# An mLSTM layer and an ELU network on one core: queries and keys as 112 rows, two small copies removed, the order made anew

## The chip, the cores and the metric

One core of a Trainium2 chip runs the whole program. The metric is device time in microseconds (us). The core has five engines with a queue each: TensorE (PE in the profile, and PEld for its weight loads), VectorE (DVE), ScalarE (ACT), GpSimd (POOL) and SyncE (SP), which here issues every transfer. Engines run side by side and wait for each other through semaphores; each works through its own list in order.

## The reference, cut to what matters

For each of 4 x 8 heads a matrix memory is updated step by step over 768 positions; its outputs, 3072 rows of 320 numbers, go through a two-layer network with an ELU between.

```python
# q, k, v, o_gate: (4, 8, 768, 40); i_gate, f_gate: (4, 8, 768)
for t in range(S):
    m_new  = np.maximum(f_gate[:, :, t] + m, i_gate[:, :, t])
    f_stab = np.exp(f_gate[:, :, t] + m - m_new)
    i_stab = np.exp(i_gate[:, :, t] - m_new)
    C = f_stab * C + i_stab * outer(v_t, k_t)          # 40 x 40 per head
    n = f_stab * n + i_stab * k_t
    y[:, :, t] = sigmoid(o_t) * (C @ q_t) / max(abs(n . q_t), 1)
x = y.transpose(0, 2, 1, 3).reshape(3072, 320)
h = x @ w_in                                          # 320 x 2048
g = np.where(h > 0, h, np.exp(np.minimum(h, 0)) - 1)
out = g @ w_out                                       # 2048 x 320
```

## The kernel before, in words

The sequence is cut into 6 chunks of 128 positions; a **tile** is one chunk of one of the 4 batches with its 8 heads, so there are 24 tiles, numbered t0 to t23. For a tile PE forms keys times queries per head (L752, two heads side by side on partitions 0 to 39 and 64 to 103, 16 matmuls). A weight matrix w holds the decays: for the first two chunks PE spreads the sums of logarithms lcs over a tile (L779 to L789, six matmuls for half the heads, "a spread") and ACT takes the exponential (L804); for later chunks DVE makes it with a scan (L796). DVE multiplies w by the products (L813). The outputs come from PE: from the second chunk on the state C times the decayed queries (L833), then w times values (L841), then the addition to the state (L851). The decay comes through DRAM: it is written as b_d and read back spread over 40 partitions into bb (L705), its last column is copied to dec (L769), and bb is multiplied by the queries in place (L770). The state shrinks by dec (L868, two instructions) and takes the addition (L879). The outputs are gated and divided into xf (L899, L903), xf's last 64 columns are copied behind it (L907), PE turns xf (L917), and it is stored as a high and a low part, xh and xl.

Two or three tiles make a **block** (9 blocks). For each block and each of 16 slices of 128 hidden columns, a **step**, PE makes h with eight matmuls (L970), ACT and DVE make the ELU and its two parts gh and gl (L978 to L988), and PE adds to acc (L997). The weights come as 64-bit words and are converted on ACT, DVE and POOL (L429 to L477); wide and narrow are their buffers. The last 64 rows of w_in of two groups share one conversion, "the tail".

Nothing runs in the order of the code. Each piece is given to a planner as an `op` with costs by engine; the planner plays the program through by these costs and a table of ranks (PLACES) and of fixed engines (USES), and writes the instructions of each engine in the order of its own start times. Where PE would stand idle in the plan before 70 us, it puts in matmuls on a tile of ones that nobody reads (L526, "fills"), one for each 0.22 us:

```python
done = self.FIRST_WORK
for t, _, e, o in order:
    if e == "PE":
        if done < t < self.WARM:
            self.fill(max(0, round((t - done - self.SLACK) / 0.22)))
        done = o.end
    o.fn(e)
```

At the very start PE gets EARLY_WORK of them ahead of anything else. The buffers of queries and keys (qk, three), of decays (bb, three) and of h (two, which spreads use as well) are taken in turn.

Of the kernel before, what the change touches and what calls it, by code (L numbers as in the profile page):

```python
# [15 lines left out]
ALU = mybir.AluOpType  # L16
# [4 lines left out]
P = 128  # L21
# [17 lines left out]
class Plan:  # L39
# [52 lines left out]
    def run(self):  # L92
# [17 lines left out]
        engines = {e: 0.0 for o in self.ops for e in o.engines}  # L110
        queue, port, t, order, events, small = 0.0, 0.0, 0.0, [], {0.0}, False
# [95 lines left out]
def tile_mlstm_then_elu_ffn(  # L207
# [9 lines left out]
    nc = tc.nc  # L217
    PSUM = bass.MemoryType.PSUM
    B, NC, _, _, _, HH, L = qk.shape
    D = 40  # L220
    DM, DFF = w_in.shape[1], w_in.shape[0] * w_in.shape[2]
# [21 lines left out]
    EARLY_WORK = 10  # L243
# [8 lines left out]
    room = dict(  # L252
        wide=3, narrow=2, gates=2, qk=3, bb=3, vko=3, w=3, wl=2, dec=2, den=2, xf=2,
        x=3, ps_a=3, h=2, acc=3, e=2, gh=4, gl=4, os=3,
    )
    PLACES = {"clear": 7.1154181, "g0": -0.805181392, "qk0": -0.351178529, "v0":
# [22 lines left out]
    USES = {"clear.2": "POOL", "rows.0": "DVE", "rows.1": "DVE", "rows.2": "DVE",  # L279
        "states.0": "ACT", "states.2": "ACT", "g0.0": "ACT", "g0.7": "DVE", "p0.4": "ACT",  # L280
        "p0.8": "DVE", "y0.6": "DVE", "y0.8": "DVE", "p1.4": "ACT", "p1.10": "POOL", "v1.1":
        "ACT", "y1.6": "ACT", "p2.10": "POOL", "v2.1": "ACT", "p3.4": "ACT", "v3.1": "ACT",
# [4 lines left out]
        "ACT", "g2.2": "DVE", "g2.4": "POOL", "g2.10": "DVE", "p8.3": "ACT", "p8.9": "ACT",  # L287
# [19 lines left out]
        "ACT", "d3.0": "ACT", "d3.1": "DVE", "c4.0": "ACT", "c5.2": "POOL", "c6.1": "ACT",  # L307
# [827 lines left out]
```

## Time and profile before

| | before |
|---|---|
| time, median of 3 runs | 470.45 us (469.73 to 471.0) |
| the profiled execution's own time | 468.6 us |
| its span, first to last instruction | 466.8 us |
| PE busy | 458.5 us, 98% |
| DVE busy | 336.5 us, 72% |
| ACT busy | 277.9 us, 60% |
| POOL busy | 100.6 us, 22% |
| transfers of SP's queue, share of 16 engines | 33.6% |

The time is that of an execution; the span is what the profile covers, 1.8 us less. Busy time counts what an engine runs, fills included, so a high share for PE does not by itself say that all of it is wanted work.

### The profile page before, as it was taken

The numbers are of one execution on the slowest core, as the hardware profiler recorded it, in microseconds if no ns is written. First come the engines' busy times: TensorE is split into PE (matmuls) and PEld (weight loads), VectorE is DVE, ScalarE is ACT, GpSimd is POOL, SyncE is SP. The second block draws the span as 40 slices with busy tenths as digits, with TensorE's granted clock in tenths as the row PEclk, the third lists the DMA queues.
The fourth block names the chain that finished last, engine by engine and source line by source line (L and its number), as shares of the span: only waits on it lengthen the run. The fifth ranks groups of instructions, "written<-read, shape, count | busy, mean of one in ns | idle before, by whom it ended". The sixth has DMA issues, their size and how long they took to land.

```text
span 466.8 us, 13897 instructions
## 1 busy us (share of the span) xinstructions
PE 458.5 (98%) x5737; PEld 429.1 (92%) x5737; DVE 336.5 (72%) x698; ACT 277.9 (60%) x672; POOL 100.6 (22%) x137
## 2 busy tenths in 40 slices
PE   9899999999999999999999999999999999999996
PEld 4557799999999999989999999999999999999996
DVE  7899899899888878778887853587894754354432
ACT  5778678788866456454654565354545455545664
POOL 1226302320212031234111340131041201010011
PEclk9999999999999999999999999999999999999999
DMA  7956374334208361246405501353411301000100
GB/s 210 317 183 198 102 276 146 114 98 148 86 8 236 103 226 41 79 131 199 144 17 150 173 1 43 114 165 119 133 45 38 95 0 44 1 3 0 44 1 28
DMA packets 42175, 49.71 MB, mean 106 GB/s; under 512 B 3360, under 2 KB 34816, under 8 KB 42112
## 3 DMA queue, kind: packets, MB, share of 16 engines
q1 hardware_dynamic: 42112, 48.82, 33.6%
q8 instruction: 45, 0.74, 0.6%
q14 instruction: 18, 0.15, 0.1%
HBM read 43.42 MB, written 5.39 MB: 105 GB/s over the span
## 4 chain that ended last, share of the span: by engine, by line
PE 96%; DVE 2%; ACT 1%; issue 1%; DVEq 0%; ACTq 0%
PE h L970 39%; PE acc L997 36%; PE ps_a L752 6%; PE ps_a L841 3%; PE ps_a L833 3%; PE acc L526 3%; PE ps_a L917 2%; PE ps_a L851 1%; PE h L779 1%; PE h L485 1%; PE h L789 1%; PE h L783 1%; DVE gl L988 0%; DVE w L477 0%; DVE w L813 0%
## 5 line engine op out<-in xcount | busy, mean ns | idle before, releaser
L970 PE MATMUL h<-xh,w 128*128 128x384 f32 (+1 forms) x720 | 176.6, 321 | 0.0
L997 PE MATMUL acc<-w,gh 128*128 128x320 f32 x768 | 172.2, 311 | 0.9 <-ACT den L886 0.7
L997 PEld LDWEIGHTS acc<-w,gh 128*128 128x128 f32 x768 | 128.9, 188 | 2.6 <-issue 0.6
L983 DVE SCALAR_TENSOR_TENSOR e<-e,h 128x384 f32<-128x384 f32 (+1 forms) x144 | 72.7, 505 | 80.6 <-ACT e L981 79.9
L970 PEld LDWEIGHTS h<-xh,w 128*128 128x128 f32 x720 | 124.6, 188 | 1.7
L978 ACT ACTIVATE e<-h 128x384 f32<-128x384 f32 (+1 forms) x144 | 65.4, 454 | 93.3 <-PE h L970 85.4
L997 PE MATMUL acc<-w,gl 128*128 128x320 f32 x384 | 118.7, 309 | 0.5 <-DVE gl L988 0.5
L970 PE MATMUL h<-xl,w 128*128 128x384 f32 (+1 forms) x432 | 111.4, 317 | 0.0
L986 ACT CAST gh<-e 128x384 fp32r<-128x384 f32 (+1 forms) x144 | 68.1, 474 | 39.6 <-DVE e L983 38.5
L970 PEld LDWEIGHTS h<-xl,w 128*128 128x128 f32 x432 | 76.3, 188 | 0.0
L988 DVE TENSOR_TENSOR gl<-e,gh 128x384 fp32r<-128x384 f32 (+1 forms) x109 | 60.6, 558 | 20.0 <-ACT gh L986 19.7
L997 PEld LDWEIGHTS acc<-w,gl 128*128 128x128 f32 x384 | 72.0, 188 | 0.9 <-DVE gl L988 0.9
L981 ACT ACTIVATE e<-e 128x384 f32<-128x384 f32 (+1 forms) x144 | 70.5, 490 | 3.6
L988 POOL TENSOR_TENSOR gl<-e,gh 128x384 fp32r<-128x384 f32 (+1 forms) x35 | 33.5, 956 | 171.2 <-ACT gh L986 125.7
L796 DVE TENSOR_TENSOR_SCAN w<-w,ident 128x512 f32<-128x512 f32 x32 | 39.4, 1241 | 1.5 <-DMA w<-f_d 1.5
L813 DVE TENSOR_TENSOR w<-ps_a,w 128x512 f32<-128x512 f32 x48 | 31.4, 683 | 2.0 <-ACT wl L342 1.0
L752 PE MATMUL ps_a<-qk 40*128 40x128 f32 x384 | 29.9, 291 | 0.3 <-DVE xl L342 0.2
L752 PEld LDWEIGHTS ps_a<-qk 40*128 40x128 f32 x384 | 25.1, 193 | 5.2 <-issue 1.8
L903 POOL TENSOR_TENSOR xf<-xf,den 128x320 f32<-128x320 f32 x13 | 10.8, 831 | 45.0 <-DVE den L891 44.6
L841 PE MATMUL ps_a<-vko,w 128*32 128x41 f32 x1536 | 19.4, 201 | 1.0 <-DVE w L813 0.9
L841 PEld LDWEIGHTS ps_a<-vko,w 128*32 128x32 f32 x1536 | 17.7, 109 | 2.2 <-DVE w L813 1.5
L868 POOL TENSOR_TENSOR C<-C,dec 40x164 f32<-40x164 f32 x20 | 10.0, 498 | 33.2 <-PE ps_a L833 27.2
(114 smaller groups left out, 432.2 us busy)
## 6 DMA issues: line engine op xcount, KB each, us to landing
w<-f_d SPq DMA_DIRECT2D x32, 256.0 KB
vko<-in_vko SPq DMA_DIRECT2D x24, 324.0 KB
qk<-in_qk SPq DMA_DIRECT2D x48, 160.0 KB
wide<-in_w_out SPq DMA_DIRECT2D x8, 640.0 KB
wide<-in_w_in SPq DMA_DIRECT2D x8, 512.0 KB
vko<-in_vko SPq DMA_DIRECT2D x24, 160.0 KB
out<-os SPq DMA_DIRECT2D x24, 160.0 KB
bb<-b_d SPq DMA_DIRECT2D x40, 80.0 KB
```

Source lines behind the costliest of these rows:

```text
L526: nc.tensor.matmul(spare, ones, ones.unsqueeze(1).to_broadcast([P, 4, P]), start=True, stop=True, skip_group_check=True,)
L752: nc.tensor.matmul(ps(two, P, HH, L)[:, j, :], kt[rows, j, :], qt[rows, j, :], start=True, stop=True,)
L796: nc.vector.tensor_tensor_scan(a, a, ident4.rearrange("p h t -> p (h t)"), 0.0, op0=ALU.mult, op1=ALU.add)
L813: lambda e, half=half: nc.vector.tensor_mul(w(half), ps(half, P, HH, L), w(half)),
L841: nc.tensor.matmul(y[r, h, :], w()[:, i, r], va()[:, h, :], start=not opened, stop=(i == H - 1), skip_group_check=True,)
L970: nc.tensor.matmul(h(), a[g][:, fs], m, start=(i == 0), stop=(i == len(prods) - 1))
L978: op(act(N), lambda e, h=h, ff=ff: nc.scalar.activation(ff("e"), h(), AF.Relu, scale=-1.0), (KHP,), (KE,))
L981: lambda e, ff=ff: nc.scalar.activation(ff("e"), ff("e"), AF.Exp, scale=-1.0), (), (KE,))
L983: lambda e, h=h, ff=ff: nc.vector.scalar_tensor_tensor(out=ff("e"), in0=ff("e"), scalar=-1.0, in1=h(), op0=ALU.add, op1=ALU.max),
L986: op(act(N), lambda e, ff=ff: nc.scalar.copy(ff("gh", F32R), ff("e")), (KE,), (KG,))
L988: lambda e, ff=ff: eng[e].tensor_sub(ff("gl", F32R), ff("e"), ff("gh", F32R).bitcast(F32)),
L997: nc.tensor.matmul(acc(a), x[:, sl], bw[g][:, j, :], start=(f == f0 and i == 0), stop=(f == f1 - 1 and i == 2),)
```

## The change

What it does: queries and keys of a tile come in one transfer of 112 rows in place of two of 40 rows; the rows 40 to 63 between the halves are zeros from DRAM, so the three memsets of qk's middle rows go. The tail of w_in comes as one transfer of 128 rows in place of two of 64. The decay times the queries is written into the queries' buffer, so bb stays whole, dec and its copy go, and the state shrinks with one instruction on 104 partitions that reads bb's last column. The gating product is written back into the gates' buffer (v3), and the division writes all 384 columns of xf at once, in the order (part, row, head); the rows of w_in are put in the same order, the copy of 64 columns goes. In the planner RATE, FIRST_WORK, EARLY_WORK, PE's start and a few costs change, and both tables are new; with them the order on all engines.

```diff
-    RATE = 255e3
+    RATE = 290e3
-    FIRST_WORK, WARM, SLACK = 5.0, 70.0, 0.1
+    FIRST_WORK, WARM, SLACK = 6.6, 70.0, 0.1
...
         engines = {e: 0.0 for o in self.ops for e in o.engines}
+        engines["PE"] = self.FIRST_WORK
...
-    EARLY_WORK = 10
+    EARLY_WORK = 13
+    W = 3 * P // (2 * H)
...
-    PLACES = {"clear": 7.1154181, "g0": -0.805181392, "qk0": -0.351178529, "v0":
-    USES = {"clear.2": "POOL", "rows.0": "DVE", "rows.1": "DVE", "rows.2": "DVE",
+    USES = {"clear.0": "DVE", "clear.1": "ACT", "clear.2": "ACT", "states.0": "DVE",
...
-                src = [w_in[x, 2 * P :] for x in (g, g + 1)]
+                src = [w_in[2 * (NF // G) + g // 2]]
...
-        op({"ACT": 0.2 + 0.00092 * n, "DVE": 0.13 + 0.0011 * n}, size, both[1::2], (KN,))
-        op({"ACT": 0.2 + 0.00092 * n, "DVE": 0.13 + 0.0011 * n}, rounding, (), both[0::2])
+        op({"ACT": 0.2 + 0.00092 * n} | one_in, size, both[1::2], (KN,))
+        op({"ACT": 0.2 + 0.00092 * n} | one_in, rounding, (), both[0::2])
...
-        plan.at("rows", rank["t0"])
-        for j, t in enumerate(qks):
-            op({"DVE": 0.52, "POOL": 0.56},
-               lambda e, t=t: eng[e].memset(t[32:64, 0], 0.0), (), (("qkzero", j),))
...
-        for x in range(2):
-            op({"SP": 0.4}, lambda e, x=x: nc.sync.dma_start(t[ROWS[x]], qk[b, c, x]),
-               (("qkzero", n % room["qk"]),), (("qk", n, x),), nbytes=D * 2 * HH * L * 4)
+        op({"SP": 0.4}, lambda e: nc.sync.dma_start(t[0:QR], qk[b, c]),
+           (), (("qk", n, 0), ("qk", n, 1)), nbytes=2 * D * 2 * HH * L * 4)
...
-            op({"POOL": 0.22, "DVE": 0.17, "ACT": 0.2},
-               lambda e: copy(e, dec(), bb[0:R2, :, L - 1 : L]), KB, (("dec", n),))
-            op(two_in(HH * L), lambda e: eng[e].tensor_mul(bb[0:R2], bb[0:R2], qt[0:R2]), KQ, KB)
+            op(two_in(HH * L), lambda e: eng[e].tensor_mul(qt[0:R2], bb[0:R2], qt[0:R2]), KB, KQ)
...
-                            y[r, 2 * j : 2 * j + 2, :], bb[0:R2, j, r], C[b][0:R2, j],
+                            y[r, 2 * j : 2 * j + 2, :], qt[0:R2, j, r], C[b][0:R2, j],
...
-                    for two, rows in enumerate(ROWS):
-                        cv = C[b][rows, :, two, :]
-                        eng[e].tensor_mul(cv, cv, dec()[rows].to_broadcast([D, HH, E]))
+                    cv = C[b][0:R2].rearrange("p j two e -> p j (two e)")
+                    eng[e].tensor_mul(cv, cv, bb[0:R2, :, L - 1 : L].to_broadcast([R2, HH, 2 * E]))
...
-        op(two_in(H * D),
-           lambda e: eng[e].tensor_mul(gated(), gated(), den().to_broadcast([P, H, D])),
-           (("den", n),), (("xf", n),))
-
-        op({"port": 1, "DVE": 0.12, "POOL": 0.25, "ACT": 0.24},
-           lambda e: copy(e, xf()[:, H * D :], xf()[:, 2 * P : H * D]), (), (("xf", n),))
+        def divided(e):
+            y = v3()[2]
+            parts, step = y.ap[0], y.ap[-1][0]
+            twice = bass.AP(
+                tensor=y.tensor, offset=y.offset,
+                ap=[parts, [D * step, H], [(D - W) * step, 2], [step, W]],
+            )
+            eng[e].tensor_mul(
+                xf().rearrange("p (a d h) -> p h a d", a=2, h=H), twice,
+                den().unsqueeze(3).to_broadcast([P, H, 2, W]),
+            )
+
+        op(two_in(3 * P), divided, (("den", n), KS), (("xf", n),))
```

The order of instructions, at three places of the start. **SP's queue**, from its first transfer (gates; vko are values, keys and output gates of a tile, wide a weight's buffer). Before:

```order
L518 DMA gatesfi<-in_gates 32x256
L677 DMA vko<-in_vko 128x648
L671 DMA qk_148<-in_qk 40x1024 x2
L682 DMA vko<-in_vko 128x320
L429 DMA wide<-in_w_in 128x512
L429 DMA wide<-in_w_in 64x512 x2
L671 DMA qk_149<-in_qk 40x1024 x2
```

The same place with the change:

```order
L522 DMA gatesfi<-in_gates 32x256
L672 DMA qk_145<-in_qk 112x1024
L683 DMA vko<-in_vko 128x320
L678 DMA vko<-in_vko 128x648
L433 DMA wide<-in_w_in 128x512 x2
L678 DMA vko<-in_vko 128x648
L672 DMA qk_146<-in_qk 112x1024
```

The first tile's queries and keys now go second, each pair of transfers is one, and the first weight is the fifth transfer in place of the sixth.

**DVE**, where the log sums of the first chunk are split into three parts (lcs) and the first weight's conversion begins (narrow<-wide). Before:

```order
L342 CAST lcs<-gateslc 32x256
L636 TENSOR_TENSOR gateslc<-gateslc,lcs 32x256
L342 CAST lcs<-gateslc 32x256
L636 TENSOR_TENSOR gateslc<-gateslc,lcs 32x256
L342 CAST lcs<-gateslc 32x256
L439 TENSOR_SCALAR narrow<-wide 128x512
```

With the change:

```order
L346 CAST lcs<-gateslc 32x256
L638 TENSOR_TENSOR gateslc<-gateslc,lcs 32x256
L346 CAST lcs<-gateslc 32x256
L443 TENSOR_SCALAR narrow<-wide 128x512
L638 TENSOR_TENSOR gateslc<-gateslc,lcs 32x256
L460 TENSOR_SCALAR narrow<-narrow 128x512
```

The conversion's first instruction, which needs the first weight, now stands ahead of the last step of the log sums, and the third cast has left DVE.

**ACT** at the same time, from the first tanh of the gates (L766) or shortly behind it, through the exponentials of the first tile (w<-h). Before:

```order
L766 ACTIVATE vko<-vko 128x320
L443 ACTIVATE wide<-wide 128x512
L804 ACTIVATE w<-h 128x512
L342 COPY wl<-w 128x4
L804 ACTIVATE w<-h 128x512
```

With the change:

```order
L346 COPY gatesm<-m_120 32x1
L447 ACTIVATE wide<-wide 128x512
L346 CAST lcs<-gateslc 32x256
L441 ACTIVATE narrow<-wide 128x512
L447 ACTIVATE wide<-wide 128x512
L800 ACTIVATE w<-h 128x512 x2
```

The third cast of lcs now stands on ACT behind one conversion instruction of the first weight, and two of the second weight stand ahead of the first tile's exponentials.

## Rows read from the trace of the kernel before

**Rows 1.** The page: span, then busy time and share by engine.
```profile
span 466.8 us, 13897 instructions
...
PE 458.5 (98%) x5737; PEld 429.1 (92%) x5737; DVE 336.5 (72%) x698; ACT 277.9 (60%) x672; POOL 100.6 (22%) x137
```

**Rows 2.** Busy us per engine by stretch (instructions), clock, DMA share, GB/s.
```profile
0.00:10.00 10.00, 8.94 (x31) 4.32 (x32) 7.06 (x24) 5.92 (x14) 1.80 (x10) 1.00 0.76 210
10.00:20.00 10.00, 9.79 (x163) 5.99 (x162) 7.97 (x17) 7.65 (x21) 2.70 (x4) 1.00 0.95 305
20.00:80.00 60.00, 57.47 (x1033) 45.78 (x1031) 54.26 (x118) 45.73 (x113) 19.44 (x27) 1.00 0.60 192
80.00:140.00 60.00, 60.00 (x502) 59.56 (x501) 54.89 (x108) 45.90 (x96) 10.51 (x13) 1.00 0.27 88
140.00:300.00 160.00, 159.20 (x2197) 154.15 (x2196) 117.70 (x244) 86.50 (x230) 39.01 (x54) 1.00 0.38 116
...
460.00:466.80 6.80, 3.12 (x19) 2.44 (x17) 1.34 (x3) 1.63 (x4) 0.74 (x1) 1.00 0.14 48
```

**Rows 3.** The chain in order of time: start us, us, engine, tile, line.
```profile
1.06 4.45 PE acc L526 x10
...
5.51 2.54 PE ps_a L752 x16
...
8.04 2.55 PE acc L526 x6
...
49.45 1.09 PE acc L526 x5
...
165.49 1.59 PE h L970 x8
...
178.65 1.39 PE h L970 x8
```

**Rows 4.** Waits of PE: us in total, times, longest.
```profile
PE ps_a L841 <- DVE w L813: 0.9, 1, 0.9
PE acc L997 <- ACT den L886: 0.7, 1, 0.7
...
PE acc L997 <- DVE gl L988: 0.5, 1, 0.5
```

**Rows 5.** Timeline, first 40 us: start us, us, engine, line, operation.
```profile
7.51 0.28 DVE L342 CAST lcs<-gateslc 32x256 bf16<-32x256 f32 x1
...
9.08 0.68 ACT L443 ACTIVATE wide<-wide 128x512 int32<-128x512 uint32 x1 [2.25 <-DMA wide<-in_w_in]
9.08 0.43 DVE L439 TENSOR_SCALAR narrow<-wide 128x512 int32<-128x512 int32 x1 [1.29 <-DMA wide<-in_w_in]
...
10.43 0.38 PE L779 MATMUL h<-mask,ident_b 128*128 128x512 bf16 x1
...
11.29 0.60 ACT L804 ACTIVATE w<-h 128x512 f32<-128x512 f32 x1 [1.52 <-PE h L789]
...
29.72 0.32 SPq L626 DMA_DIRECT2D b_d<-gatesfi  x1
...
38.40 0.19 POOL L342 COPY dec<-bb 104x4 f32<-104x4 f32 x1 [0.36 <-DMA bb<-b_d]
```

**Rows 6.** Groups by line and form: busy us, mean ns, idle before.
```profile
L903 DVE TENSOR_TENSOR xf<-xf,den 128x320 f32<-128x320 f32 x11 | 5.3, 485 | 0.2
...
L868 DVE TENSOR_TENSOR C<-C,dec 40x164 f32<-40x164 f32 x12 | 4.5, 377 | 0.2
...
L342 ACT COPY xf<-xf 128x64 f32<-128x64 f32 x16 | 3.8, 236 | 3.3 <-DVE xf L903 2.1 <-POOL xf L903 1.2
...
L575 DVE MEMSET qk<- x3: 485/485/485, 1.2 to 2.2; 32x512 f32 x3
```

**Rows 7.** The tile qk: ns min/median/max, first and last start us.
```profile
L752 PE MATMUL ps_a<-qk x384: 266/272/579, 5.4 to 410.7; 40*128 40x128 f32 x192
...
L671 SPq DMA_DIRECT2D qk<-in_qk x48: 281/310/1127, 1.7 to 349.5; - x48
```

More of the change, by code (lines that the diff above doesn't have):

```diff
@@ L218, in tile_mlstm_then_elu_ffn @@
     PSUM = bass.MemoryType.PSUM
-    B, NC, _, _, _, HH, L = qk.shape
+    B, NC, QR, _, HH, L = qk.shape
     D = 40
-    DM, DFF = w_in.shape[1], w_in.shape[0] * w_in.shape[2]
+    DM, DFF = out.shape[1], w_out.shape[0] * w_out.shape[1] * w_out.shape[2]
     H, S = 2 * HH, NC * L
@@ L252, in tile_mlstm_then_elu_ffn @@
     room = dict(
-        wide=3, narrow=2, gates=2, qk=3, bb=3, vko=3, w=3, wl=2, dec=2, den=2, xf=2,
+        wide=3, narrow=2, gates=2, qk=3, bb=3, vko=3, w=3, wl=2, den=2, xf=2,
         x=3, ps_a=3, h=2, acc=3, e=2, gh=4, gl=4, os=3,
     )
-    PLACES = {"clear": 7.1154181, "g0": -0.805181392, "qk0": -0.351178529, "v0":
[22 rows of a table removed]
-    USES = {"clear.2": "POOL", "rows.0": "DVE", "rows.1": "DVE", "rows.2": "DVE",
-        "states.0": "ACT", "states.2": "ACT", "g0.0": "ACT", "g0.7": "DVE", "p0.4": "ACT",
-        "p0.8": "DVE", "y0.6": "DVE", "y0.8": "DVE", "p1.4": "ACT", "p1.10": "POOL", "v1.1":
-        "ACT", "y1.6": "ACT", "p2.10": "POOL", "v2.1": "ACT", "p3.4": "ACT", "v3.1": "ACT",
[4 rows of a table removed]
-        "ACT", "g2.2": "DVE", "g2.4": "POOL", "g2.10": "DVE", "p8.3": "ACT", "p8.9": "ACT",
[19 rows of a table removed]
-        "ACT", "d3.0": "ACT", "d3.1": "DVE", "c4.0": "ACT", "c5.2": "POOL", "c6.1": "ACT",
[5 rows of a table removed]
-        "ACT", "c17.0": "ACT", "c17.5": "DVE", "d17.0": "DVE", "f.5": "DVE", "f.12": "DVE",
[20 rows of a table removed]
-        "DVE", "f.1018": "POOL", "f.1039": "POOL", "f.1053": "DVE", "f.1060": "POOL",
-        "f.1067": "POOL"}
+    PLACES = {"m0": 7.89582482, "clear": 5.23509032, "states": 7.06301, "gl0": -1.63453576,
[27 rows of a table added]
+    USES = {"clear.0": "DVE", "clear.1": "ACT", "clear.2": "ACT", "states.0": "DVE",
+        "states.1": "DVE", "states.3": "POOL", "g0.0": "ACT", "v0.1": "ACT", "p1.4": "ACT",
+        "y1.5": "ACT", "y1.7": "ACT", "p2.4": "ACT", "p2.10": "POOL", "y2.5": "ACT", "p3.4":
+        "ACT", "p3.8": "ACT", "g1.9": "DVE", "p4.2": "DVE", "p4.9": "DVE", "p5.2": "DVE",
+        "p5.5": "ACT", "p5.9": "ACT", "y5.3": "DVE", "p6.2": "DVE", "p6.5": "ACT", "v6.1":
+        "POOL", "y6.5": "ACT", "p7.2": "POOL", "p7.5": "ACT", "y7.3": "DVE", "g2.0": "ACT",
[17 rows of a table added]
+        "DVE", "c1.2": "POOL", "d1.0": "ACT", "d2.0": "ACT", "d2.1": "DVE", "d2.3": "POOL",
+        "c3.2": "DVE", "d3.0": "ACT", "c4.0": "ACT", "c4.1": "ACT", "c4.2": "DVE", "c4.5":
+        "DVE", "c5.1": "ACT", "d5.0": "ACT", "c6.0": "DVE", "c6.2": "POOL", "d6.0": "ACT",
+        "d6.2": "ACT", "c7.0": "ACT", "c7.1": "ACT", "c7.2": "POOL", "d7.0": "ACT", "c8.0":
+        "DVE", "c8.1": "ACT", "c8.2": "POOL", "c8.5": "DVE", "d8.0": "ACT", "c9.2": "POOL",
[25 rows of a table added]
+        "POOL", "f.1076": "DVE", "f.1078": "DVE"}
     plan = Plan(room, ("qk", "bb", "e", "gh", "gl", "os"))
@@ L393, in tile_mlstm_then_elu_ffn @@
                 conv_of_1[g].append(len(convs))
-                convs.append(([w_in[g, t * P : (t + 1) * P]], [(slice(0, P), w1h[t][g], w1l[t][g])], G * P, f))
+                convs.append(([w_in[2 * g + t]], [(slice(0, P), w1h[t][g], w1l[t][g])], G * P, f))
             if g % 2 == 0:
@@ L534, in setup @@
         busy_work(EARLY_WORK)
+        plan.at("m0", -9.0)
         op({"DVE": 0.1}, lambda e: nc.vector.memset(m0, -1e30), (), (("m0", 0),))
+        plan.at("setup", 0.0)
         op({"POOL": 1.6}, lambda e: make_identity(nc, ident), (), (("ident", 0),))
@@ L555, in setup @@
         op({"POOL": 0.6}, masked, (), (("mask", 0),))
-        op({"POOL": 0.7, "DVE": 0.6},
-           lambda e: eng[e].tensor_copy(ident4, ident.unsqueeze(1).to_broadcast([P, HH, L])),
+        op({"POOL": 0.7, "ACT": 0.62},
+           lambda e: copy(e, ident4, ident.unsqueeze(1).to_broadcast([P, HH, L])),
            (("ident", 0),), (("ident4", 0),))
@@ L706, in load @@
                    (("b_d", c), ("bbzero", (n - B) % room["bb"])), (("bb", n - B, two),),
-                   nbytes=D * HH * L * 4)
+                   nbytes=64 * HH * L * 4)
     def attention(n, rank):
@@ L865, in shrink @@
                 def shrink(e):
-                    for two, rows in enumerate(ROWS):
-                        cv = C[b][rows, :, two, :]
-                        eng[e].tensor_mul(cv, cv, dec()[rows].to_broadcast([D, HH, E]))
-                op({"port": 1, "POOL": 1.06, "DVE": 0.6}, shrink, (("dec", n),), (("C", b),))
+                    cv = C[b][0:R2].rearrange("p j two e -> p j (two e)")
+                    eng[e].tensor_mul(cv, cv, bb[0:R2, :, L - 1 : L].to_broadcast([R2, HH, 2 * E]))
+                op({"port": 1, "POOL": 0.85, "DVE": 0.49}, shrink, KB, (("C", b),))
             def gather(e):
@@ L893, in attention @@
         op({"port": 1, "DVE": 0.41}, denominators, (), (("den", n),))
-        def gated():
-            return xf()[:, 0 : H * D].rearrange("p (h d) -> p h d", d=D)
         op({"DVE": 0.49},
            lambda e: nc.vector.scalar_tensor_tensor(
-               out=gated(), in0=v3()[2], scalar=1.0, in1=y3()[:, :, 0:D], op0=ALU.add, op1=ALU.mult),
-           (KY, KS), (("xf", n),))
-        op(two_in(H * D),
-           lambda e: eng[e].tensor_mul(gated(), gated(), den().to_broadcast([P, H, D])),
-           (("den", n),), (("xf", n),))
-        op({"port": 1, "DVE": 0.12, "POOL": 0.25, "ACT": 0.24},
-           lambda e: copy(e, xf()[:, H * D :], xf()[:, 2 * P : H * D]), (), (("xf", n),))
+               out=v3()[2], in0=v3()[2], scalar=1.0, in1=y3()[:, :, 0:D], op0=ALU.add, op1=ALU.mult),
+           (KY,), (KS,))
+        def divided(e):
[10 more added lines that the diff above has]
+        op(two_in(3 * P), divided, (("den", n), KS), (("xf", n),))
         kb, slot = where[n]
@@ L917, in turn @@
                 nc.tensor.matmul(
-                    ps("tp", P, 3, L)[:, t, :], xf()[:, t * P : (t + 1) * P], ident,
+                    ps("tp", P, 3, L)[:, t, :], xf()[:, -t % 3 * P : (-t % 3 + 1) * P], ident,
                     start=(t == 0), stop=(t == 2), is_transpose=True, skip_group_check=True,
@@ L1103 @@
     t = np.transpose
+    rows = [40 * h + d for d in (*range(16), *range(24, 40), *range(16, 24)) for h in range(8)]
+    w_in = t(moe_w_in.view(np.int64)[rows].reshape(320, 4, 512), (1, 0, 2))
     arrays = {
         "qk": np.ascontiguousarray(
-            t(np.stack([q, k]).reshape(2, 4, 4, 2, 6, 128, 40), (1, 4, 3, 6, 0, 2, 5))
+            np.pad(
+                t(np.stack([q, k]).reshape(2, 4, 4, 2, 6, 128, 40), (1, 4, 3, 6, 0, 2, 5)),
+                [(0, 24) if x == 3 else (0, 0) for x in range(7)],
+            ).reshape(4, 6, 128, 2, 4, 128)[:, :, 0:112]
         ),
@@ L1117 @@
         ),
-        "w_in": np.ascontiguousarray(t(moe_w_in.view(np.int64).reshape(320, 4, 512), (1, 0, 2))),
+        "w_in": np.concatenate(
+            [w_in[:, 0:256].reshape(8, 128, 512), w_in[:, 256:].reshape(2, 128, 512)]
+        ),
         "w_out": np.ascontiguousarray(
```

4 lines of the change are left out of this document (1 added, 3 removed), and 139 rows, old and new, of tables (PLACES, USES).

## The prediction, made before the changed kernel ran

> **What bounds the kernel now.** I read the page's first lines, then the table of stretches, the chain, PE's waits, and last the timeline of the first 40 us. The page [rows 1] has PE busy for 458.5 of 466.8 us, so the first question is what PE's remaining 8.3 us are, and the second what of its busy time is not wanted work. The table of stretches [rows 2] places the idle time: 1.06 us at the very start, 0.21 from 10 to 20 us, 2.53 from 20 to 80, nothing from 80 to 140, 0.80 from 140 to 300, and 3.68 in the last 6.8 us, where the last sums are copied and sent out. So behind the start and ahead of the end PE idles 3.5 us in all. The reader should see the other engines in the same rows: DVE is busy for 54.3 of 60 us from 20 to 80 and for 54.9 from 80 to 140, but only for 117.7 of 160 after that. The early stretch is one in which DVE paces PE; later PE alone sets the pace.
>
> What is busy but not wanted shows in the chain [rows 3]. PE begins with ten fills, 4.45 us, or 0.445 us each; the first products follow (2.54 us for 16 matmuls), then six more fills, 2.55 us. Later five fills take 1.09 us, 0.22 each. The first stretch's row prints a granted clock of 1.00 [rows 2], which is the 2.4 GHz level, but the same fill comes at half the pace there; I take the pace of the chain. The order of instructions has 47 fills, so 31 come at 0.22 us. The span is then wanted PE work, plus fills, plus waits, plus the two ends, and a change is worth what it takes from the last three. All the wanted matmuls are in both orders in equal number and form, so their sum drops out.
>
> **The change part by part.** *The start of PE.* The order now has 14 fills ahead of the first products (13 fixed, one put in by the planner) and three behind them, where ten and six stood. At the slow pace the 14 end at 1.06 + 14 x 0.445 = 7.3 us, the products at 9.8, three fills of 0.425 at 11.1, where the six ended at 10.6 [rows 3]: 0.5 us late. If the pace doubled at 7.3 us, PE would be through by 9.1 and would wait for the log sums. They were complete at 7.51 + 0.28 us before [rows 5]; now DVE does the first weight's 0.43 us instruction ahead of them, and that weight landed at 9.08 us. With it, the last subtraction and the cast on ACT, each taken at 0.43 too, the spread begins at 10.4 against 10.43 [rows 5]: no gain. With hops I keep -0.1 and +0.5 as ends and take +0.1, nearer to the lower, since the weight's landing holds both cases.
>
> *The first weight's landing.* It was sixth in SP's queue behind 836 KB and is now fifth behind 964, since the padded rows travel too (448 KB for a tile's queries and keys, 320 before). At the 305 GB/s of the stretch from 10 to 20 us [rows 2] 128 KB more are 0.42 us; that would put the spread at 10.8, inside the ends just given. The Trainium skill (DMA: Bandwidth & Descriptors, the section on why a DMA increments its semaphore by 16) says that a transfer runs on the largest number of engines up to 16 that divides its rows: 10 for 40 rows, 16 for 112. By that the busiest engine has 28 KB of such a tile in place of 32, and the weight would land some 0.1 us earlier in place of 0.42 later; no row here shows the engines apart.
>
> *Fills.* 35 later fills in place of 31, at 0.22 us: +0.9 us. The planner puts them where its own plan has PE idle, so they are PE time spent either way; they cost nothing only where PE would wait there in fact.
>
> *Runs of small matmuls.* A step's eight matmuls take 1.59 us right behind a run of products and 1.39 elsewhere [rows 3]. In the order I count 40 unbroken runs of products and outputs before and 42 now: 2 x 0.2 = +0.4 us; at the least 0, if the joins fall on fills.
>
> *Waits.* DVE loses three memsets of 0.485 us at the start, the second instruction of each shrinking (0.377 each; one of 104 x 328 elements should take the 0.485 us of the 128 x 320 division), and some copies of xf; most of those copies were ACT's, 16 of 0.236 us [rows 6]. It gains divisions: 18 of 24 are on DVE, where 11 were, each of 384 columns and by elements some 0.56 us. I counted the instructions on DVE ahead of the tenth ELU instruction (L983) in both orders and priced each by its mean in the view by line and form: 72.1 us before and 67.9 now. The yardstick gives 367.6 us for all of DVE where the page has 336.5, so the difference is about 3.8 us. PE's waits on DVE by name, 0.9 us for w and 0.5 for gl [rows 4], should go with that: -1.4. The wait on ACT (0.7) I leave. A new one comes: the second weight's two ACT instructions of 0.68 us now stand ahead of the first exponentials. That weight lands 512 KB behind the first, 1.7 us at 305 GB/s, so at 10.8; the exponential starts at 12.2 in place of 11.29 [rows 5]. The third spread needs one of the two h buffers back and waits for it; of the 0.9 us two fills, put in just there, cover 0.4: +0.5. In all PE's 3.5 us of waits become 2.6: -0.9. The ends are none at all (-3.5), and 3 us more (+3.0), the case of the slower rivals below.
>
> *Hidden.* A qk buffer is now held until the outputs and not only until the multiplication, so SP can wait longer on a load, and what is queued behind it (values, bb, weights) with it. Cover: the last load was issued at 349.5 us and its products began no earlier than about 410 [rows 7]; gone, it would cost PE the wait itself. 24 + 2 fewer issues of 0.31 us [rows 7] lie on SP alone. The end is the same but for both last copies on DVE, one behind the other: 0.1 us, left out.
>
> **The sum.** +0.1 +0.9 +0.4 -0.9 = +0.5 us. The profiled execution's span becomes 467.3 us and its time, 1.8 us more, 469.1. That execution was 1.85 us faster than the median of the three runs, 470.45; the difference carries over: 470.95, I say 470.9.
>
> **The rivals.** I call it no change within 0.3% (1.4 us), about what a measurement of this kernel can tell from none.
>
> *Faster: DVE's 3.8 us come out whole.* PE then waits for nothing behind the start: -0.1 + 0.9 + 0 - 3.5 = -2.7, 467.75 us. For it speaks that DVE paced PE from 20 to 140 us [rows 2]; against it that PE's list has more fills than before, which no engine's haste takes out. With the other terms as taken, it decides when PE's waits between 10 and 460 us fall under 0.7 us.
>
> *Slower: the division's columns.* It now writes each head's numbers 8 elements apart, 32 bytes. No row here has such a write: the ends are the 0.485 us of the plain one [rows 6], with 0.56 by elements, and twice that. At 1.1 us the first tiles' divisions, three on DVE and one on POOL, add some 2 us to the engine that paces PE: 472.9 us. It decides from about 0.9 us each. The Trainium skill (Advanced Engine Details and Errata, SBUF Cachelines) says that accesses which each touch another 16-byte line pay a penalty, and by that this rival would hold; it gives no price.
>
> *Slower: the decay through DRAM.* Before, b_d went out at 29.72 us and bb was there at 38.40 [rows 5], 8.7 us later. Now its exponential stands on ACT behind the second tile's xl, which I place at 31 us, so 39.8 by the same trip. The first outputs from a state now follow the first step at once, about 40.5 us. DVE's multiplication by the queries waits for bb, behind it on DVE the products' weighting and the first ELU, and PE waits for both. Beyond 39.8 each us costs one: at 42, 2.2 us, so 473.1. For it: nothing in that order can pass it. Against: fewer transfers stand between b_d and bb on SP.
>
> **How the numbers follow.** No change 0.52, faster 0.25, slower 0.23 (0.10 the columns, 0.13 the decay). The likeliest is 470.9 us. Its own range, with the start and the runs at their ends and the waits from 1.5 to 4.0 us, is -0.1 + 0.9 + 0 - 2.0 = -1.2 to +0.5 + 0.9 + 0.4 + 0.5 = +2.3: 469.2 to 472.8. The whole range reaches to the faster rival, 467.7, and past the slower ones to the upper end of the waits, +0.1 + 0.9 + 0.4 + 2.0 = +3.4: 473.8.
>
> **What would show it.** The profile of the changed kernel should have 52 fills, 17 of them at about 0.43 us, the first spread between 10.3 and 11.1 us, the first exponential near 12.2, the first step (L970) some 1 to 2 us earlier than in the trace of before, hardly a wait of PE on DVE's gl from 50 to 140 us, and PE's waits between 10 and 460 us near 2.6 us in all. I am wrong if fills come at the fast pace from 7 us on and the spread begins earlier than 10 us, if the division takes over 0.9 us, or if PE waits several us ahead of its first outputs from a state.

## The result, and the profile after

The changed kernel takes 476.39 us (475.05 to 477.08, 4 runs) against 470.73 us (469.73 to 472.2, 4 runs) for the one before: ratio 1.0108, 95% interval 1.0072 to 1.0143. The forecast was 470.9 us, no change; the measured time lies above the forecast's upper end of 473.8.

The page of the changed kernel, span and busy times; they answer to [rows 1]:

```profile
span 475.3 us, 13810 instructions
PE 463.9 (98%) x5742; PEld 431.1 (91%) x5742; DVE 339.4 (71%) x674; ACT 274.0 (58%) x645; POOL 104.5 (22%) x125
```

The span is 8.5 us longer, more than the medians differ by, since the profiled execution of before was 2.1 us under its median (468.6) and this one 0.7 over (477.08). PE is busy 5.4 us more and idle 3.1 us more. The stretches, with the columns of [rows 2], place the idle time:

```profile
0.00:10.00 10.00, 6.73 (x34) 2.94 (x34) 5.77 (x21) 5.01 (x12) 2.42 (x12) 1.00 0.75 246
10.00:20.00 10.00, 9.42 (x149) 5.66 (x150) 6.98 (x16) 7.42 (x17) 2.76 (x5) 0.83 1.06 313
20.00:80.00 60.00, 58.99 (x1066) 46.18 (x1069) 53.94 (x110) 45.58 (x110) 20.13 (x23) 1.00 0.60 186
80.00:140.00 60.00, 59.96 (x485) 58.46 (x474) 54.13 (x105) 44.15 (x95) 8.56 (x10) 1.00 0.45 145
140.00:300.00 160.00, 156.90 (x2149) 150.41 (x2149) 126.62 (x250) 84.63 (x217) 40.92 (x47) 0.99 0.40 117
```

From 20 to 80 us PE idles 1.01 us, where it idled 2.53: the early gain that the forecast counted on came. But between 140 and 300 us it idles 3.10 us, where it idled 0.80, and in the first 20 us 2.8 us beside the 1.05 before the first fill, where it was 0.2. Two single waits make nearly all of that. PE's waits (us in total, times, longest), the answer to [rows 4]:

```profile
PE h L970 <- DVE e L983: 2.9, 1, 2.9
PE h L779 <- ACT lcs L346: 2.6, 1, 2.6
```

The first of them, by the timeline (start, duration, what):

```profile
275.57 1.34 SPq L696 DMA_DIRECT2D w<-f_d  x2
...
276.21 0.48 DVE L891 SCALAR_TENSOR_TENSOR vko<-vko,ps_a 128x320 f32<-128x320 f32 x1
...
276.95 0.49 SPq L672 DMA_DIRECT2D qk<-in_qk  x1
...
277.61 0.93 DVE L902 TENSOR_TENSOR xf<-vko,den 128x384 f32<-128x384 f32 x1
...
278.60 0.35 SPq L678 DMA_DIRECT2D vko<-in_vko  x1
...
285.99 0.50 DVE L761 TENSOR_TENSOR vko<-vko,iT 128x328 f32<-128x328 f32 x1 [2.48 <-DMA vko<-in_vko]
286.30 0.47 ACT L764 ACTIVATE vko<-vko 128x320 f32<-128x320 f32 x1 [2.06 <-DMA vko<-in_vko]
```

and the chain in order of time behind it:

```profile
278.60 7.30 DMA vko<-in_vko
...
286.89 0.47 DVE e L983
...
287.41 2.93 PE h L970 x8
```

Tile t19's values can only be loaded when the division of tile t16 has left the buffer (278.54 us). In the kernel before, the gating (here L891, done at 276.69 us) was the last to read that buffer. But SP was busy with other issues until 277.44 us, so the longer hold delays this load by 1.2 us at most. The transfer takes 7.30 us, behind 512 KB of decays and 448 KB of queries and keys that were issued in the 3 us ahead of it. DVE's weighting of these values (L761) and ACT's tanh (L764) stand at the head of their queues and keep them idle for 2.48 and 2.06 us, the ELU behind them, and PE waits 2.93 us for e. Then PE's next eight matmuls take 2.93 us where they take 1.39: the granted clock of the stretch is 0.74, so part of it ran at the lower of the two levels, 1.2 GHz in place of 2.4. The same stretch, PE alone (us, busy, clock, DMA share, GB/s):

```profile
280.00:285.00 5.00, 4.48 (x29) 1.00 0.53 159
285.00:290.00 5.00, 2.59 (x8) 0.74 0.01 2
290.00:295.00 5.00, 5.00 (x29) 0.92 0.05 16
```

In all 4.5 us at this one place, in this execution (2.93 of waiting and 1.5 of slower matmuls). The start, the answer to [rows 5]:

```profile
1.05 4.67 PE L530 MATMUL acc<-ones 128*128 128x512 bf16 x14 [1.05 <-DVE m L540]
5.65 1.16 PE L750 MATMUL ps_a<-qk 40*128 40x128 f32 x16
...
7.40 0.38 PE L775 MATMUL h<-mask,ident_b 128*128 128x512 bf16 x1
...
9.04 0.43 DVE L443 TENSOR_SCALAR narrow<-wide 128x512 int32<-128x512 int32 x1 [2.19 <-DMA wide<-in_w_in]
9.50 0.41 DVE L638 TENSOR_TENSOR gateslc<-gateslc,lcs 32x256 f32<-32x256 f32 x1
9.94 0.40 ACT L346 CAST lcs<-gateslc 32x256 bf16<-32x256 f32 x1 [0.23 <-DVE gateslc L638]
10.40 0.39 PE L779 MATMUL h<-sel,lcs 96*128 96x512 bf16 x1 [2.62 <-ACT lcs L346]
```

The first spread begins at 7.40 us with its matmul on the mask, which needs no log sums; its second matmul (L779) waits for the last part of lcs until 10.40. Behind this wait too the granted clock fell: it is 0.50, the 1.2 GHz level, from 12 to 14 us, where the kernel before has 1.00.

The last thing is seen only in the chain of a late stretch, where PE does nothing but steps: 16 first-layer matmuls of 256 columns, or of 384, in a row. Before:

```profile
443.60 1.88 PE h L970 x16
```

After (445.89 shows that the second layer keeps its pace, 1.76 us for 12, as it had before):

```profile
443.97 1.92 PE h L970 x16
445.89 1.76 PE acc L997 x12
...
352.20 2.80 PE h L970 x16
```

Behind 140 us, pieces of 16 with 384 columns are 2.77 or 2.78 us in 16 of 18 cases before; after, 10 of 17 are 2.80 or 2.81 and five 2.78 or 2.79. That is 0.020 us per step of two tiles and up to 0.015 per step of three, and with 48 and 96 steps up to 2.4 us.

### The profile page after: what moved, and what is told of

The parts are those of the page before. It is cut to its first block, busy times and chain, and to the rows that moved or that the text cites. A ratio compares the mean times of both kernels' runs of the same rounds, so it can differ in the third digit from the quotient of the medians.

```text
span 475.3 us, 13810 instructions
## 1 busy us (share of the span) xinstructions
PE 463.9 (98%) x5742; PEld 431.1 (91%) x5742; DVE 339.4 (71%) x674; ACT 274.0 (58%) x645; POOL 104.5 (22%) x125
## 4 chain that ended last, share of the span: by engine, by line
PE 88%; DMA 5%; DVE 3%; ACT 2%; issue 1%; SPq 0%; DVEq 0%; ACTq 0%
PE h L970 37%; PE acc L997 35%; PE ps_a L750 5%; DMA vko<-in_vko 3%; PE ps_a L829 3%; PE ps_a L837 3%; PE ps_a L917 1%; DMA wide<-in_w_in 1%; PE ps_a L847 1%; PE h L779 1%; PE h L785 1%; PE h L775 1%; PE acc L530 1%; DVE e L983 1%; PE h L489 0%
## 5 line engine op out<-in xcount | busy, mean ns | idle before, releaser
L970 PE MATMUL h<-xh,w 128*128 128x384 f32 (+1 forms) x720 | 178.7, 324 | 2.9 <-DVE e L983 2.9
L970 PEld LDWEIGHTS h<-xh,w 128*128 128x128 f32 x720 | 126.4, 190 | 5.1 <-DVE e L983 3.5
L970 PE MATMUL h<-xl,w 128*128 128x384 f32 (+1 forms) x432 | 113.0, 320 | 0.0
L988 POOL TENSOR_TENSOR gl<-e,gh 128x384 fp32r<-128x384 f32 (+1 forms) x53 | 51.9, 985 | 191.9 <-ACT gh L986 154.8
L970 PEld LDWEIGHTS h<-xl,w 128*128 128x128 f32 x432 | 77.8, 190 | 0.0
L988 DVE TENSOR_TENSOR gl<-e,gh 128x384 fp32r<-128x384 f32 (+1 forms) x91 | 50.2, 553 | 19.4 <-ACT gh L986 19.1
L750 PE MATMUL ps_a<-qk 40*128 40x128 f32 x384 | 28.8, 285 | 0.1
L750 PEld LDWEIGHTS ps_a<-qk 40*128 40x128 f32 x384 | 24.0, 187 | 4.2 <-issue 2.8
L764 ACT ACTIVATE vko<-vko 128x320 f32<-128x320 f32 x24 | 11.1, 466 | 17.3 <-DMA vko<-in_vko 17.2
L813 POOL TENSOR_TENSOR vko<-vko,wl 128x320 f32<-128x320 f32 x16 | 13.3, 832 | 31.6 <-ACT wl L346 10.4
```

What stands on the lines that cost most here:

```text
L750: nc.tensor.matmul(ps(two, P, HH, L)[:, j, :], kt[rows, j, :], qt[rows, j, :], start=True, stop=True,)
L970: nc.tensor.matmul(h(), a[g][:, fs], m, start=(i == 0), stop=(i == len(prods) - 1))
L988: lambda e, ff=ff: eng[e].tensor_sub(ff("gl", F32R), ff("e"), ff("gh", F32R).bitcast(F32)),
```

## The experiments

The order that the planner made was written out as a list, so that one place can be changed and the rest stays. Ratios are to the kernel before, run beside it. In a_same, a_late19, a_plain and a_start line numbers are 33 lower than in the changed kernel.

**a_same**: the list alone, no edit.

> The changed kernel once more, its order of instructions written out as a list so that single places of it can be edited. If the 2.93 us wait of PE for e (L983) near 285 us and the 1.5 us of slower matmuls behind it belong to the order and the transfers, they come again, and the median stays within 1 us of 476.4. If they were an accident of the one profiled execution, they are missing here and the median comes out nearer to 472.

1.0116 (1.0073 to 1.0160). The median, 478.24 us, is 1.8 us above the 476.4 expected, but the kernel before, run beside it, is also 1.6 us higher (472.32), so the ratio is the one to read. The wait is there again (2.76 us in front of the matmul at 288.34 us, clock 0.73 from 290 to 295). It belongs to the program, though its length is not the same in every execution, as a_start2 shows below.

**a_late19**, DVE's list (ACT's tanh moves alike):

```diff
 TENSOR_TENSOR xl<-ps_a,xh 128x3x128
-TENSOR_TENSOR vko<-vko,iT 128x328
-TENSOR_TENSOR vko<-vko,wl 128x320
 SCALAR_TENSOR_TENSOR e<-e,h 128x384
...
-TENSOR_TENSOR vko<-vko,iT 128x328
+TENSOR_TENSOR vko<-vko,iT 128x328 x2
+TENSOR_TENSOR vko<-vko,wl 128x320
```

> Tile t19's weighting of values (L761, with L813) on DVE and its tanh (L764) on ACT stand some 6 us later in their lists, behind tile t18's weighting; all else as in the changed kernel. Theory A (both stand in their queues ahead of ELU work while their transfer, issued at 278.6 us, lands only at 285.9): the wait of 2.93 us and the 1.5 us of slower matmuls behind it go, 476.4 - 4.4 = 472.0 us, 471 to 473. Theory B (the late release of the buffer by the division and the load itself are what counts): PE meets the same late tile a little later, and the gain stays under 1 us, 475.4 to 476.4.

1.0042 (1.0008 to 1.0076). 0.74% or 3.5 us less than a_same, near theory A's 4.4; with both intervals the difference is 0.74% give or take 0.55. The stretch is full and at full clock:

```profile
285.00:290.00 5.00, 5.00 (x31) 1.00 0.06 16
```

**a_plain**: the division writes its columns one behind the other.

```diff
-xf().rearrange("p (a d h) -> p h a d", a=2, h=H), twice,
+xf().rearrange("p (h a d) -> p h a d", a=2, h=H), twice,
```

> The division writes its 384 columns one behind the other instead of 8 apart (the same numbers in another place, so the network's input has its columns in another order than the rows of w_in). Theory B (the division's strided write costs PE the time): a division on DVE falls from 0.90 to about 0.56 us, and the buffer that t19's load waits for comes free sooner; with DVE's 18 divisions 6 us less, the median falls by 3 us or more, to 473 or below. Theory A: the divisions get shorter, but the wait near 285 us shrinks by no more than the 0.35 us by which the load is issued earlier, and the median by under 1 us: 475.4 to 476.4. If the write has no price, a division stays at 0.9 us and nothing moves.

The rows of w_in keep their order here, so this kernel does the same work but leaves out what would make its numbers right. 1.0085 (1.0052 to 1.0119). The division's row (L869 is L902), min, median and max in ns; first of the changed kernel, then of a_plain:

```profile
L902 DVE TENSOR_TENSOR xf<-vko,den x18: 849/899/1037, 19.5 to 426.1; 128x384 f32<-128x384 f32 x18
```

```profile
L869 DVE TENSOR_TENSOR xf<-vko,den x18: 519/554/736, 17.9 to 423.6; 128x384 f32<-128x384 f32 x18
```

The stride costs 0.345 us a division, 6.2 us of DVE. The ratio is 0.3% under a_same's, some 1.5 us, which is within the noise of the two. The wait near 285 us is still 2.6 us long; in this profile the clock did not fall behind it.

**a_start**: first weight's L443, L447 and L455 behind the first chunk's log sums.

```diff
-g0.9:DVE c1.1:ACT c1.0:DVE g0.10:DVE o1.0:SP c1.2:POOL g0.11:ACT
+g0.9:DVE g0.10:DVE o1.0:SP g0.11:ACT c1.1:ACT c1.0:DVE c1.2:POOL
```

(g0 is the first chunk's gates, c1 the first weight's conversion, each with the number of the step and its engine.)

> The first weight's first instructions on DVE (L443), ACT (L447) and POOL (L455) stand behind the log sums of the first chunk instead of ahead of their end. The log sums are then complete near 7.3 us in place of 10.34. If PE's wait of 2.62 us for them is lost time, the first spread begins near 7.9 us and the median falls by 2 to 3.5 us, to 473 to 474.4. If DVE and ACT pace PE from there on, the time is given back by 60 us: within 1 us of 476.4.

1.0095 (1.0066 to 1.0124): within noise of a_same. The wait for log sums is gone, but the third spread waits 2.2 us for an exponential (L800) behind ACT's L447, which waits for the weight. So one wait of PE was put in place of another, and the clock fell behind it as well (0.50 from 12 to 18 us).

**a_start2**: exponentials and weighted products of the first tile go ahead of both weights too.

```diff
-c1.1 c1.0 c1.2 c1.3 c2.0 c1.4 p0.6 c2.1 c2.2 p0.3 c1.5 p0.7 p0.4 p0.5 d1.0 p0.8 p0.10 p0.9
+p0.6 p0.3 p0.7 p0.4 p0.5 p0.8 p0.10 p0.9 c1.1 c1.0 c1.2 c1.3 c2.0 c1.4 c2.1 c2.2 c1.5 d1.0
```

> The changed kernel with the first tile's whole chain (log sums, exponentials L800, weighted products L809) ahead of the first and second weight's conversions on DVE, ACT and POOL. The first spread should begin near 7.5 us and the third should no longer wait for an exponential behind the weights, which cost 2.2 us in a_start. If the start's wait of 2.6 us is time lost for good, the ratio falls by 0.4% or more against 1.0116; if DVE paces PE from there and the conversions only come later, PE waits as much for other things until 60 us and the ratio stays within 0.2%.

1.0111 (1.0069 to 1.0153): no gain against a_same that can be seen, with an uncertainty of 0.6%. The trace shows the waits elsewhere (1.5, 1.1, 1.0 us for other things). So nothing was won by moving the start's wait; that it costs nothing is not shown, since no run is free of such waits.

This trace shows one thing more. Nothing was edited near 285 us, yet t19's values took only 5.42 us to load, and PE waited 1.08 us, with no fall of the clock behind it. In six other executions of this order with t19's load and work unchanged (the changed kernel, a_same, a_plain, a_start, a_pad64, a_all64) the load took 7.10 to 7.41 us and the wait 2.6 to 3.1. So the wait differs between executions, and one profile with a shorter wait does not show that an edit shortened it.

**a_pad64 and b_pad64**: in the changed kernel and in the one before,

```diff
-return T("wl", n, P, H)
+return T("wl", n, P, 2 * H)[:, 0:H]
```

> Without the tile dec every tile behind it in the local memory moved 64 bytes down. Here the tile wl is made 32 bytes wider (two buffers), so that x, e, gh, gl and os lie at the addresses of the kernel before; order and work are those of the changed kernel. Theory C (PE reads x more slowly from the new addresses): a first-layer matmul of 256 columns takes 117 ns again instead of 120, the first five of 384 columns 174 in place of 177, in all about 48 x 8 x 2.7 + 96 x 12 ns = 2.2 us, and the median falls by 0.4 to 0.5%. Rival (another cause of the 3 ns, or none): they stay at 120 and 177 ns and the median stays within 0.2% of the changed kernel's.

1.0034 (1.0011 to 1.0056), and the chain's pieces are those of before:

```profile
441.77 1.88 PE h L970 x16
```

> The kernel before in its own order, with wl widened alike, so that x, e, gh, gl and os lie 64 bytes higher than in it (and 128 higher than in the changed kernel). Theory C with the address modulo 128 as what counts: first-layer matmuls of 256 columns take 120 ns here, and the kernel is some 0.4 to 0.5% slower than the kernel before. If only the very addresses of the changed kernel are slow, or the address is not the cause, they stay at 117 ns and the ratio at 1.000.

1.0071 (1.0045 to 1.0097), and the old kernel now has the slow pieces:

```profile
442.06 1.92 PE h L970 x16
```

From ends of matmuls in the records: 256 columns mostly take 117 ns in the kernel before and in a_pad64, 120 in the changed kernel, 119 to 121 in b_pad64. Summed from end to end, all first-layer matmuls take 184.38 us in a_plain and 182.03 in a_pad64, neither of which lost clock near 285 us: 2.35 us, 0.5%, which the intervals of both kernels allow.

**a_all64**:

```diff
+const.tile([P, 16], F32, name="gap")
 w1 = [const.tile([P, 5, G * P], F32R, name=f"w1{g}") for g in range(NF // G)]
```

> The changed kernel with 64 bytes left free ahead of the weights w1, so that w1 and x both move by 64 bytes: x lies where it lay in the kernel before, but its distance to w1, which PE loads meanwhile, is that of the changed kernel. If x's own address modulo 128 is what counts, the 256-column matmuls of the first layer take 117 ns as in a_pad64 and the ratio falls to 1.003. If the distance between x and w1 counts (both are read at once), they stay at 120 ns and the ratio at 1.0116.

1.0079 (1.0053 to 1.0105), between a_same's and a_pad64's; its ratio alone would not decide, the matmuls do: 120 ns, pieces of 1.92 us (448.69 us). The profiled execution took 481.82 us, but the granted clock is 1.00 from 445 to 455 us, so the piece can be compared.

```profile
448.69 1.92 PE h L970 x16
```

x lies here where it lay before, and is slow, and w1 moved with it. So x's own address does not decide; where it lies against w1, the other tile that these matmuls read, fits all four cases. That it is w1, and not one of the tiles between the two, which moved along, is argued from what the matmuls read.

**a_late_pad**: a_late19 and a_pad64 together.

> Both edits: tile t19's weighting and tanh later, and the 64 bytes put back. If theories A (late transfer at the head of two queues, measured at 0.74%) and C (addresses, 0.4 to 0.5%) hold and are independent, the ratio to the kernel before comes out at 1.0116 - 0.0074 - 0.0045 = 0.9997, no difference. If C fails, it stays near 1.004.

1.0009 (0.9984 to 1.0035), the span 468.4 us: with two edits no difference to the kernel before is left.

**a_heads_inner**: a_late_pad with the division's loops turned.

```diff
-ap=[parts, [D * step, H], [(D - W) * step, 2], [step, W]],
+ap=[parts, [(D - W) * step, 2], [step, W], [D * step, H]],
...
-xf().rearrange("p (a d h) -> p h a d", a=2, h=H), twice,
+xf().rearrange("p (a d h) -> p a d h", a=2, h=H), twice,
...
```

> a_late_pad with the division's loops turned: heads innermost, so that it writes its 384 columns one behind the other and reads the gated outputs 40 numbers apart; the result is the same numbers at the same places. If only a strided write is dear, a division on DVE takes about 0.56 us as in a_plain and the ratio falls by 0.2 to 0.3% below a_late_pad's 1.0009, to about 0.998. If a strided read costs as much, it stays at 0.9 us and the ratio at 1.0009.

0.9988 (0.9959 to 1.0018), not to be told from a_late_pad. A read of numbers 160 bytes apart costs what the write 32 bytes apart did, and POOL more (0.986 us became 1.226):

```profile
L902 DVE TENSOR_TENSOR xf<-vko,den x18: 856/908/989, 19.3 to 423.4; 128x384 f32<-128x384 f32 x18
```

**a_nofill**: `self.fill(n)` left out of the list.

> The changed kernel with only the 13 fixed fills at the start; the planner's 39 later ones, 35 of them taken as PE time of 0.22 us, are left out. If they stand where PE would wait anyway, as the planner means them, PE waits longer by what they took (8 us) and the ratio stays within 0.2% of 1.0116. If they are time spent on top, as the prediction's sum took them, the median falls by up to 8 us, to 0.995. If they keep PE's clock up, as well as covering waits, the ratio rises.

1.0221 (1.0183 to 1.0258), median 482.0 us: 1.05% slower than a_same. Beside a_same's profile, without 39 fills PE runs 9.5 us less of them (14.05 to 4.52), idles 5.6 us more, and its wanted work takes 9.8 us longer. The granted clock of that execution is 0.972 against 0.996. So these fills were worth 5 us and not a cost.

**a_qk80**:

```diff
-lambda e: nc.sync.dma_start(t[0:QR], qk[b, c]),
+lambda e: [nc.sync.dma_start(t[r], qk[b, c][r]) for r in (ROWS if n > 2 else [slice(0, QR)])],
```

> From the fourth tile on, queries and keys come again as two transfers of 40 rows, without the 32 padding rows that the single transfer carries (128 KB of 448 for a tile). If the padding is what makes tile t19's values land late, the wait near 285 us shrinks by the 0.44 us that 128 KB take at 290 GB/s, or more, and the ratio falls by 0.1 to 0.6%. If the padding is hidden, the wait keeps within 0.3 us of 2.9 and the ratio within 0.15% of 1.0116; 21 more issues of 0.31 us on SP cost nothing.

1.0013 (0.9989 to 1.0037), 1.03% less than a_same: more than expected. The wait near 285 us is 1.45 us and the clock stays at 1.00. t19's values load from 275.37 in 6.09 us, not from 278.60 in 7.30:

```profile
275.37 6.09 DMA vko<-in_vko
```

But most of these 3.2 us were gained earlier: the queries and keys of the tile before go out at 264.66 us already, where the changed kernel has 267.60. And a load in 5.42 us comes in a_start2 too, with all the padding. So the ratio shows what the padding costs, but this wait does not show where.

**a_qk80_early**: the same for `2 < n < 16` only.

> The changed kernel with 80 rows for tiles t3 to t15 and 112 rows for t16 to t23. If the 1.03% that a_qk80 gained comes from the first half (the start, where transfers run at 300 GB/s), the ratio falls to about 1.003; if it comes from tile t19's late landing, the wait near 285 us stays at 2.9 us and the ratio at 1.009 to 1.0116.

1.0014 (0.9984 to 1.0044): by the ratio the gain comes with tiles t3 to t15. The profiled execution (474.99 us, the median is 472.9) also shows t19's wait at 1.46 us, though t19 itself is padded: its load takes 5.69 us there, from 279.56.

**b_qk112**: the kernel before, with padded queries and keys in DRAM.

```diff
-nc.sync.dma_start(t[ROWS[x]], qk[b, c, x]),
+x or nc.sync.dma_start(t[0:QR], qk[b, c]),
```

> The kernel before, in its own order, with each tile's queries and keys as one transfer of 112 rows (448 KB for 320, 24 issues fewer on SP). Theory D (the padding costs by itself, 3.1 MB more through the queues): slower by 0.5 to 1%. Rival (it costs only where the new order puts a tile's work right behind its loads): within 0.2% of the kernel before.

0.9997 (0.9963 to 1.0031): no cost that can be seen. The padding costs only together with the new order.

**a_three**: a_late_pad and a_qk80.

> All three edits that moved the time: queries and keys as two transfers of 40 rows from the fourth tile on (1.03% alone), the 64 bytes put back (0.8%), tile t19's weighting and tanh later (0.74%). The first and the third act on the same wait near 285 us, so they don't add: if the padding costs only through that wait, the ratio stays at a_late_pad's 1.001 or at 1.0013 - 0.008 = 0.993 at best. If it costs along the whole kernel, the ratio comes out at 0.993 or below, faster than the kernel before by 0.5% or more.

0.9943 (0.9921 to 0.9964), median 469.24 against 472.04 us: faster than both kernels. It is 0.66% (give or take 0.33) under a_late_pad, where the wait near 285 us is gone already. So the padding costs something elsewhere too. Page and waits:

```profile
span 467.8 us, 13855 instructions
PE 458.5 (98%) x5742; PEld 426.7 (91%) x5742; DVE 340.5 (73%) x674; ACT 272.8 (58%) x645; POOL 103.8 (22%) x125
...
PE 90%; DMA 4%; DVE 2%; ACT 2%; SPq 1%; issue 1%; DVEq 0%; ACTq 0%
```

```profile
PE h L779 <- ACT lcs L346: 1.5, 1, 1.5
...
PE h L970 <- DVE e L983: 0.9, 2, 0.7
```

## Why the forecast was wrong

**The step that failed first is "Hidden".** It said that a buffer held longer costs PE nothing, and took as cover one load, the last, issued at 349.5 us for products at 410 [rows 7]. That cover was read in the old order. In the new one tile t19 is loaded at 278.60 us and worked on at 285.99, 7.4 us later; in the kernel before its values were loaded at 299.36 us, 20 us later in the program. The step looked at queries and keys only; the buffer that this load waited for was that of values and output gates, which the division now reads to its end. The hold is the smaller part, 1.2 us at most; the rest belongs to the new order, which puts t19's work so soon behind its load, and to the traffic ahead of it; how much to each is not shown. And the 128 KB of padding were costed for the first weight alone (0.42 us, hidden) and not for 24 tiles, though they are 3.1 MB. The planner, too, was told 320 KB for such a transfer of 448 (nbytes in the change) when it made the order; what order it makes with 448 was not tried. The page's shares of the chain show what that did, first before, then after:

```profile
PE 96%; DVE 2%; ACT 1%; issue 1%; DVEq 0%; ACTq 0%
```

```profile
PE 88%; DMA 5%; DVE 3%; ACT 2%; issue 1%; SPq 0%; DVEq 0%; ACTq 0%
```

No transfer was on the chain before; 5% of it are transfers now. This share alone proves little, since a_three has 4% and is the fastest of all. The experiments decide: a_late19 gives back 3.5 us by moving t19's instructions, a_qk80 4.8 us by less traffic. The two overlap in part, as a_three shows.

**The second step that failed** is the sentence that the wanted matmuls' sum "drops out" because they are equal in number and form. Without fills, and each matmul counted from the end of the one before it, PE's work takes 444.5 us in the profile before and 450.4 in that after. The first layer has 3.6 us of the difference: 1.5 are the fall of the clock near 285 us; the other 2.1 are about what the address is worth. The second layer has 2.0 us more, the products 1.2 less. The address is a cost that the sum did not have at all. dec was named as a removed copy; that it is also 64 bytes of memory, by which x moves against w1, was not seen. It is worth 2.35 us by the matmuls of a_plain and a_pad64, and its effect is shown in both directions (a_pad64, b_pad64).

**Waits** (3.5 to become 2.6 us): DVE's part was right, PE's waits from 20 to 140 us fell from 2.53 to 1.05 us. The wait that the third spread was to bring (+0.5) did not come: the first exponential began at 11.69 us, not 12.2, and two fills were enough. But the waits near 285 us and of the start came. Between the first fill and the last 15 us PE idled 6.9 us (11.36 in the span, less 1.05 at the start and 3.37 at the end). The range was also too narrow by its own terms: this step gives 3 us more as the upper end of the waits, but the whole range adds only 2.0 for them. With 3.0 it would have reached 474.9 us, still under the measured time.

**The start** (+0.1): the time of the spread was right by luck. The spread's matmul that needs the log sums came at 10.40 as worked out, with the weight landing at 9.04 us. But the 14 fills ran in 4.67 us, not 6.2, since their pace doubled at about 4.3 us; the spread began at 7.40 with its matmul on the mask, and PE waited 2.62 us. So both things came that the prediction named as signs that it is wrong here: fast fills and a spread begun before 10 us. Even so the first step (L970) began 0.9 us earlier, at 40.20 in place of 41.11 us, close to the 1 to 2 us foretold. Two experiments that moved this wait gained nothing that can be measured, and both have other waits in its place. The larger transfers ahead of the weight cost nothing that can be seen: it landed at 9.08 us before, and between 8.36 and 9.33 in the eight traces of this order that leave the start as it is (the changed kernel, a_same, a_late19, a_plain, a_pad64, a_all64, a_late_pad, a_heads_inner). The Trainium skill's rule on engines per transfer (DMA: Bandwidth & Descriptors, the section on why a DMA increments its semaphore by 16), cited above, had said 0.1 earlier; the rows are nearer to that than to 0.42 later, but they spread too widely to bear it out.

**Fills** (+0.9): the sign was wrong. The 52 fills take 13.6 us in all where 47 took 14.0, since more of them ran at the fast pace. a_nofill shows that the 39 that the planner put in save 5 us in all; a term of so many fills by 0.22 us is no cost where PE would wait and lose its clock. **Small runs** (+0.4) were not tested apart.

**The rivals.** *Faster* fell with the waits. *The division's columns*: the price was at its deciding point, 0.899 us, but it decides little: taking the stride away gives 0.3%, no more than the noise, and why not more was not tried apart. The trace agrees in direction with the Trainium skill's rule (Advanced Engine Details and Errata, SBUF Cachelines), cited above: 0.554 us became 0.899, and 0.908 for a strided read. *The decay through DRAM* did not happen: DVE's first multiplication started at 39.9 us as worked out, and PE waited for none.

**What stays open.** The three parts give back 0.74, 0.8 and 1.03% one by one and 1.73% together (1.0116 to 0.9943), so they overlap by some 0.9%, with an uncertainty about as large. Together they give back more than the whole difference of the two kernels (1.16%), but the split is not exact. Where the padding costs its time, and why that of tiles t3 to t15 seems to be what matters, is not shown by any single wait; nor is it why t19's load takes 5.4 us in some executions and over 7 in others. Nor was the second layer's wait near 125 us tried, where DVE's gl takes 1.98 us in place of its median 0.55 beside POOL's L481 (1.28 us) and PE loses 0.9 us in every run of this order.

## What to carry to other kernels

Cover for a held buffer is read per buffer and at its tightest tile, in the new order: find the load with the least time between issue and first use, and see what stands behind that use on its engine. Removing a tile also moves every tile behind it; a step that repeats a thousand times should be compared at its own pace in a stretch with no waits, where 3 ns a matmul can be seen. Padding that rides along cost nothing in one order of this kernel and 0.7 to 1% in another, so it is tried in the order that will run.

## What was not expected of the hardware

First-layer matmuls took 120 ns in place of 117 (256 columns) when x lay a multiple of 128 bytes from w1 in the program's addresses, and 117 when it lay 64 bytes beside that: x at 181184 and w1 at 16512 is fast, 181120 or 181248 and 16512 slow, 181184 and 16576 slow again. The second layer did not change, 1.76 us for 12, though gh and gl moved alike. The wait of 2.6 to 3.1 us near 285 us was followed by a fall of the granted clock, to 0.67 to 0.82 in the lowest 5 us, in four of six executions (the changed kernel, a_same, a_start, a_all64; not a_plain and a_pad64), and one of 1.08 to 1.46 us by none in three (a_start2, a_qk80, a_qk80_early). At the start a wait of 2.05 to 2.62 us was followed by 0.50, the 1.2 GHz level, from 12 to 14 us in all five executions that had one (the changed kernel, a_start, a_all64, a_late_pad, a_heads_inner), and one of 1.31 to 1.62 us by none in seven (a_same, a_late19, a_plain, a_pad64, a_qk80, a_qk80_early, a_three).
